# A decay-attention and two-expert-layer kernel: where TensorE is set back by one block, and when attention outputs leave PSUM

## The chip, the cores and the metric

The kernel runs on one core of a Trainium2 chip. The metric is the device time of one execution in microseconds (us); the figure for a kernel is the median of its runs. The core has five engines that work side by side, each through its own instructions in program order: TensorE (PE in the rows; PEld is its weight load), VectorE (DVE), ScalarE (ACT), GpSimd (POOL) and SyncE (SP), which here only issues the loads. They wait for one another through semaphores. SBUF is the working memory, PSUM the memory that TensorE writes.

## What is computed

An attention with a per-channel decay, then two mixture-of-experts layers on its output. Only the attention concerns us; cut to what matters:

```python
# q, k, v, f_logit: (4, 8, 768, 48)
f = 1.0 / (1.0 + np.exp(-f_logit))
for t in range(S):
    state = f[:, :, t, :, None] * state + np.einsum('bhd,bhe->bhde', k[:, :, t], v[:, :, t])
    y[:, :, t] = np.einsum('bhd,bhde->bhe', q[:, :, t], state)
x = attn_out.transpose(0, 2, 1, 3).reshape(3072, 384)
x = moe(x)      # expert = argmax of the gate logits, capacity 768, relu(x w1) w2
x = moe2(x)     # the same without capacity, with an output gate
```

## The kernel before

The attention is done in chunks of 128 positions. A **block** is one chunk of one batch with all 8 heads: 4 batches of 6 chunks, 24 blocks, numbered from 0. `c` is the chunk within its batch (block number modulo 6); the state that is carried from chunk to chunk is reset at c = 0 and not passed on at c = 5. Every block goes through these steps:

- `load(i)`: SyncE issues the load of the decays, q and k of block i into `fqk` (four buffers, so a load waits until block i-4 no longer needs its buffer, that is for kh(i-4)), and of v into `vt`.
- `decays(i)` and `starts(i)`: ScalarE takes the sigmoid of the block's decays into `f0` (line 605) and of each chunk's first position into `d1` (line 609).
- `elem(i)`: VectorE scans the running products `Pt` (line 615), takes a reciprocal, scans backward to `Qt` (line 622), and multiplies `qh` (line 627); GpSimd multiplies `kh` (line 630). Between them `tick` puts small VectorE jobs that route earlier groups of four blocks to experts (lines 316 to 354).
- `pe1(b)`: TensorE makes the scores of block b (line 638) and transposes kh (line 642); ScalarE copies both out of PSUM (`AT`, line 646, two copies; `kT`, line 649); GpSimd masks `AT` (line 647).
- `pe2(b)`: TensorE sums y (lines 660 and 676) and the state (lines 667 and 670); VectorE scales the state (`St`, line 679); ScalarE copies y out of PSUM to `yT` (line 682).
- `pe3(b)`: TensorE turns yT into token rows and gate logits (line 694); ScalarE copies the rows (`xrow`, line 695), VectorE reduces the logits (line 534).

One loop over i = 0 to 27 (iterations, counted from 0) writes these down, and the order in which they are written is the order on each engine (a manual schedule). Iteration i holds, in this order: `load(i+2)`, `elem(i)`, `decays(i+1)`, splits of expert weights that are due, then for the block `b` that the next line picks `pe1(b)`, `starts(i+1)`, `pe3(b-2)`, `pe2(b-1)`; then GpSimd's scatters of routed rows, and in the last iterations the transposes `xj` of the first expert's rows.

```python
b = i - 1 if i <= LAG else NBLK + 2 if i == LAG + 1 else i - 2
```

So TensorE first follows `elem` by one block; in iteration LAG+1 it gets no block at all; after that it follows by two. With `LAG = 3` the empty iteration is i = 4. TensorE's own order (block after block pe1, pe3, pe2) doesn't depend on LAG; what depends on it is where the ScalarE, VectorE and GpSimd instructions of these steps stand among those of `elem` and `decays`.

After the loop the rows of the first expert go through `layers` (lines 1065 and 1093), and the rest of the kernel is expert layers, TensorE work almost throughout.

Of the kernel before, what the change touches and what calls it, by code (L numbers as in the profile page):

```python
# [51 lines left out]
PMIN = 1e-30  # L52
PTHR = 1e-20
GROUP = 4
LAG = 3
CHOOSE, MEASURE = 2, 3
PACE, PACE2, TAIL, TAIL1 = (4, 2, 4, 4), (10, 3, 4, 4), (12, 0), (1, 4)
WT0, XT0 = (8, 10), [9, 9, 9]
# [7 lines left out]
def moe_attention_kernel(ctx: ExitStack, tc, blk, vblk, iw1, iw2, w1a, w2a, w1b, w2b, cap, out):  # L66
    nc = tc.nc
    V, A, G, PE = nc.vector, nc.scalar, nc.gpsimd, nc.tensor
# [31 lines left out]
    def psum_y(shape):  # L100
        return py.tile(shape, F32, name="pys", tag="pys")

    def psum_t(shape):
        return pt.tile(shape, F32, name="ptr", tag="ptr")
# [65 lines left out]
    def consts_load():  # L170
        nc.sync.dma_start(out=iw1_s, in_=iw1)
        nc.sync.dma_start(out=cap_i, in_=cap[0:1, 0:1].to_broadcast([128, 1]))
# [73 lines left out]
    def tick(n=1):  # L246
        for _ in range(n):
            if bg and not hasattr(bg[0], "on_pe"):
                bg.pop(0)()

    def tick_pe():

        if bg and hasattr(bg[0], "on_pe") and not bg[0].on_pe:
            bg.pop(0)()

    def tick_end():
        if bg and hasattr(bg[0], "on_pe"):
            bg[0].on_pe = False
# [283 lines left out]
    def attention():  # L542
        with ExitStack() as ac:
# [31 lines left out]
            st = {}  # L575
# [3 lines left out]
            def pace():  # L579
                return 4 if now[0] >= NBLK else 2 if rush or len(bg) > 12 else 1  # L580

            def load(i):
                t = Slot()
                x = ap.tile([HD, 3 * 512], F32, name="fqk", tag="fqk", bufs=4)
                t.v = ap.tile([128, 512], F32, name="vt", tag="vt", bufs=6)
                if i > 3:
                    nc.sync.dma_start(out=x, in_=blk[i])
                else:
                    for j in range(3):
                        nc.sync.dma_start(out=x[:, j * 512:(j + 1) * 512], in_=blk[i, :, j * 512:(j + 1) * 512])  # L590
                t.f, t.q, t.k = (x[:, j * 512:(j + 1) * 512] for j in range(3))
                st[i] = t
                if i:
                    load_v(i - 1)
                if i == NBLK - 1:
                    load_v(i)

            def load_v(i):
                nc.sync.dma_start(out=st[i].v, in_=vblk[i])

            def decays(i):
                t = st[i]
                ff = f0[i % 2]
                f4 = t.f.rearrange("p (a b) -> p a b", b=C)
                A.activation(out=ff[:, :512].rearrange("p (a b) -> p a b", b=C)[:, :, 1:],
                             in_=f4[:, :, 1:], func=AF.Sigmoid)

            def starts(i):
                A.activation(out=d1[:, 0::C], in_=st[i].f[:, 0::C], func=AF.Sigmoid)

            def elem(i):
                t = st[i]
                ff = f0[i % 2]
                Pt = ap.tile([HD, 512], F32, name="Pt", tag="Pt")
                V.tensor_tensor_scan(out=Pt, data0=ff[:, :512], data1=d1, initial=0.0,  # L615
                                     op0=ALU.mult, op1=ALU.add)
                tick(pace())
                t.pc = pcs[:HD, i * NP:(i + 1) * NP]
                V.tensor_scalar(out=t.pc, in0=Pt[:, C - 1::C], scalar1=PMIN, scalar2=None, op0=ALU.max)
                V.reciprocal(out=d1[:, ::-1][:, C - 1::C], in_=t.pc)  # L620
                Qt = ap.tile([HD, 512], F32, name="Qt", tag="Qt")
                V.tensor_tensor_scan(out=Qt[:, ::-1], data0=ff[:, 512:0:-1], data1=d1,
                                     initial=0.0, op0=ALU.mult, op1=ALU.add)
                tick(pace())
                t.qh = ap.tile([HD, 512], F32, name="qh", tag="qh", bufs=4)
                t.kh = ap.tile([HD, 512], F32, name="kh", tag="kh", bufs=3)
                V.tensor_tensor(out=t.qh, in0=t.q, in1=Pt, op=ALU.mult)  # L627
                tick(pace())

                (V if i < 2 else G).tensor_tensor(out=t.kh, in0=t.k, in1=Qt, op=ALU.mult)  # L630
# [21 lines left out]
            def pe2(i):  # L652
                t = st[i]
                c = i % NC
                S0, S1 = St[i % 2], St[(i + 1) % 2]
                y = psum_t([HD, NP, C])
                for p in range(NP):
                    for h in range(2):
                        u = 2 * p + h
                        PE.matmul(y[h * 64:h * 64 + (64, D)[h], p], lhsT=t.v[:, u * 64:u * 64 + (64, D)[h]],  # L660
                                  rhs=t.AT[h][:, p], start=(p == 0), stop=(c == 0 and p == NP - 1))
                heads = [(h, slice(h * 64, h * 64 + D), slice(h * 64, h * 64 + (64, D)[h])) for h in range(2)]
                if c < NC - 1:
                    sp = psum_y([HD, NP, D])
                    if c:
                        for h, hs, hw in heads:
                            PE.matmul(sp[hw], lhsT=ident[:HD, hw], rhs=S0, start=True, stop=False)
                    for p in range(NP):
                        for h, hs, hw in heads:
                            PE.matmul(sp[hw, p], lhsT=t.kT[:, p, hw],  # L670
                                      rhs=t.v[:, (2 * p + h) * 64:(2 * p + h) * 64 + D],
                                      start=(c == 0 and p == 0), stop=(p == NP - 1))
                if c:
                    for p in range(NP):
                        for h, hs, hw in heads:
                            PE.matmul(y[hs, p], lhsT=S0[hs, p], rhs=t.qh[hs, p * C:(p + 1) * C],  # L676
                                      start=False, stop=(p == NP - 1))
                if c < NC - 1:
                    V.tensor_tensor(out=S1, in0=sp, in1=t.pc.unsqueeze(2).to_broadcast([HD, NP, D]), op=ALU.mult)
                tick(pace())  # L680
                t.yT = ap.tile([HD, NP, C], F32, name="yT", tag="yT")
                A.copy(t.yT, y)

            def pe3(i):
                t = st[i]
# [60 lines left out]
            starts(0)  # L746
            decays(0)
            load(1)
            for i in range(NBLK + 4):
                now[0] = i  # L750
                if 2 <= i + 2 < NBLK:
                    load(i + 2)
                if i < NBLK:
                    elem(i)
                if i + 1 < NBLK:
                    decays(i + 1)
                if i == 0:
                    consts_load()
                if i < len(consts):
                    consts[i]()  # L760

                due = [p for p in wj if p[0] <= i]
                del wj[:len(due)]
                for _, f in due:
                    f()
                b = i - 1 if i <= LAG else NBLK + 2 if i == LAG + 1 else i - 2
                if 0 <= b < NBLK:
                    pe1(b)
                if i + 1 < NBLK:
                    starts(i + 1)  # L770
                tick_pe()
                if 0 <= b - 2 < NBLK:
                    pe3(b - 2)
                if 0 <= b - 1 < NBLK:
                    pe2(b - 1)
                if i >= hold:
                    scatters(2)
                if xj and i >= sincx:
                    xj.pop(0)()
                due = [p for p in wl if p[0] <= i]  # L780
                del wl[:len(due)]
                for _, f in due:
                    f()
                if ready.get("w") == i - 1:
                    steps = [0, 1, 2, 3, 4, 4, 5, 5, 6, 6, 7, 7]
                    wl = [(i + n, f) for n, f in zip(steps, W[0](0, 6) + W[0](1, 6))]
                    wj = [(i + n + 2, f) for n, f in zip(steps, split_jobs(0))]
                if ready.get("z") == i - 1:
                    early1.zeros(next(rows1), 5)
                if ready.get("x") == i - 1:  # L790
                    sincx = hold = i + 2
                    state["early"] = early1.rows(xs1, xearly)
                    xj = xt_jobs(state["early"])
                if i == NBLK:
                    flag()
                tick_end()
# [83 lines left out]
    class Plan:  # L880
# [143 lines left out]
        def next(self):  # L1024
            for t in (self.thr, self.row0, self.wrow):
                V.tensor_copy(self.turn, t)
                V.tensor_copy(t[:, :NOV - 1], self.turn[:, 1:])
# [408 lines left out]
```

## Time and profile before

| what | us |
|---|---|
| three timed runs | 635.26, 633.57, 635.64 |
| their median | 635.26 |
| the profiled execution's own time | 634.44 |
| its span, first to last instruction | 632.6 |
| busy in it: TensorE | 601.0 (95%) |
| VectorE | 394.0 (62%) |
| ScalarE | 319.8 (51%) |
| GpSimd | 160.3 (25%) |

The profiled execution is 0.82 us under the median, and 1.84 us of its time lie outside its span. The attention fills roughly the first 143 us of the span, and expert layers the rest. A busy TensorE in the profile is not the same as one at its peak; in the attention its instructions start back to back over long stretches, and that is what counts here. All positions below are us from the span's start.

### The profile page before, as it was taken

What the parts mean: (1) busy time and instruction counts of PE and PEld (TensorE: products, weight loads), DVE (VectorE), ACT (ScalarE), POOL (GpSimd) and SP (SyncE); (2) the same over time, 40 slices, a digit from 0 to 9 for tenths busy, and PEclk for the clock granted to TensorE, in tenths of its full rate; (3) what the DMA queues carried; (4) which work ended last, traced back from release to release, by engine and by line L of the source; (5) the groups of instructions that cost most, each with busy time, mean ns of one, the idle gap of its engine ahead of it and who ended that gap; (6) DMA issues with size and microseconds to landing.
All of it is one profiled execution on the core that took longest, in us unless ns stands there. A gap on an engine that the chain in (4) does not pass through costs nothing.

```text
span 632.6 us, 13955 instructions
## 1 busy us (share of the span) xinstructions
PE 601.0 (95%) x5240; PEld 579.9 (92%) x5240; DVE 394.0 (62%) x1075; ACT 319.8 (51%) x722; POOL 160.3 (25%) x219
## 2 busy tenths in 40 slices
PE   7799999988899999999999999999999999999990
PEld 7689888878899999999999999999999999999990
DVE  7778899947667474847567684544544454764520
ACT  3456665654545454544546354254554464665530
POOL 2556887655110102021120201120111010110120
PEclk9979999999999999999999999999999999999996
DMA  8997888548386273554554551285545344855210
GB/s 238 224 232 214 241 239 222 205 143 311 118 255 208 87 227 126 194 164 155 172 176 137 162 190 35 58 311 177 193 169 170 127 161 154 255 202 183 93 38 14
DMA packets 31532, 110.34 MB, mean 174 GB/s; under 512 B 4109, under 2 KB 15154, under 8 KB 27614
## 3 DMA queue, kind: packets, MB, share of 16 engines
q1 hardware_dynamic: 26158, 95.05, 49.4%
q0 software_dynamic: 5296, 14.30, 6.9%
q8 instruction: 43, 0.70, 0.5%
q14 instruction: 35, 0.29, 0.2%
HBM read 83.47 MB, written 26.21 MB: 173 GB/s over the span
## 4 chain that ended last, share of the span: by engine, by line
PE 51%; issue 29%; DVE 7%; POOL 5%; DMA 4%; ACT 2%; SPq 0%; POOLq 0%; DVEq 0%; ACTq 0%
PE pys L1093 18%; PE phs L1065 12%; PE pxs L1065 6%; POOL out L377 4%; DMA fqk<-blk 2%; PE ptr L660 2%; PE ptr L694 2%; PE phs L638 2%; PE ptr L676 2%; DVE Pt L615 2%; PE ptr L1115 1%; PE pys L1115 1%; PE phs L508 1%; DVE qh L627 1%; PE pys L670 1%
## 5 line engine op out<-in xcount | busy, mean ns | idle before, releaser
L1093 PE MATMUL pys<-hbuf,w2h 128*128 128x360 f32 (+10 forms) x864 | 206.5, 321 | 0.0
L1093 PEld LDWEIGHTS pys<-hbuf,w2h 128*128 128x128 f32 x864 | 149.8, 188 | 1.1
L1093 PE MATMUL pys<-hbuf,w2l 128*128 128x360 f32 (+10 forms) x432 | 137.8, 319 | 0.0
L377 POOL DMA_INDIRECT xs<-xrow,r_dest x53 | 55.0, 1038 | 204.3 <-DVE xl L510 85.9
L1065 PE MATMUL phs<-xh,w1h 128*128 128x312 f32 (+10 forms) x306 | 99.6, 325 | 1.7 <-DVE xl L510 1.0
L1065 PE MATMUL phs<-xl,w1h 128*128 128x312 f32 (+10 forms) x306 | 96.7, 316 | 0.0
L1065 PE MATMUL phs<-xh,w1l 128*128 128x312 f32 (+10 forms) x306 | 96.7, 316 | 0.0
L233 DVE TENSOR_TENSOR w2l<-raw,w2h 128x512 fp32r<-128x512 f32 x96 | 65.6, 687 | 45.6 <-ACT w2h L232 44.9
L233 DVE TENSOR_TENSOR w1l<-raw,w1h 128x512 fp32r<-128x512 f32 x96 | 65.3, 696 | 30.2 <-ACT w1h L232 29.6
L1093 PEld LDWEIGHTS pys<-hbuf,w2l 128*128 128x128 f32 x432 | 81.5, 189 | 0.5
L377 POOL DMA_INDIRECT out<-xrow,oid x31 | 30.3, 977 | 183.7 <-ACT xrow L1165 174.6
L1068 DVE SCALAR_TENSOR_TENSOR hbuf<-phs,hbuf 128x312 fp32r<-128x312 f32 (+10 forms) x102 | 50.8, 499 | 23.1 <-ACT hbuf L1067 22.2
L1067 ACT ACTIVATE hbuf<-phs 128x312 fp32r<-128x312 f32 (+10 forms) x102 | 46.1, 452 | 34.7 <-PE phs L1065 33.8
L1065 PEld LDWEIGHTS phs<-xh,w1h 128*128 128x128 f32 x306 | 57.7, 188 | 2.7 <-DVE xl L510 1.3
L232 ACT CAST w2h<-raw 128x512 fp32r<-128x512 f32 x96 | 59.3, 623 | 0.0
L232 ACT CAST w1h<-raw 128x512 fp32r<-128x512 f32 x96 | 57.7, 621 | 1.0 <-DMA raw<-w1a 1.0
L1065 PEld LDWEIGHTS phs<-xl,w1h 128*128 128x128 f32 x306 | 57.7, 189 | 0.4
L1065 PEld LDWEIGHTS phs<-xh,w1l 128*128 128x128 f32 x306 | 57.7, 189 | 0.3
L1099 ACT COPY ybuf<-pys 128x312 f32<-128x312 f32 (+4 forms) x27 | 11.7, 435 | 73.5 <-PE pys L1093 73.5
L1096 ACT CAST ybuf<-pys 128x360 fp32r<-128x360 f32 (+5 forms) x27 | 12.3, 455 | 72.2 <-PE pys L1093 72.2
L1065 PE MATMUL pxs<-xh,w1h 128*128 128x360 f32 (+10 forms) x150 | 48.8, 325 | 0.0
L1065 PE MATMUL pxs<-xl,w1h 128*128 128x360 f32 (+10 forms) x150 | 47.6, 317 | 0.0
(236 smaller groups left out, 1052.0 us busy)
## 6 DMA issues: line engine op xcount, KB each, us to landing
fqk<-blk SPq DMA_DIRECT2D x20, 672.0 KB, 5.6
raw<-w1b SPq DMA_DIRECT2D x8, 1536.0 KB, 7.9
raw<-w2b SPq DMA_DIRECT2D x8, 1536.0 KB, 6.9
raw<-w1a SPq DMA_DIRECT2D x7, 1536.0 KB
raw<-w2a SPq DMA_DIRECT2D x7, 1536.0 KB, 8.3
vt<-vblk SPq DMA_DIRECT2D x24, 256.0 KB, 7.2
xs<-zrow SPq DMA_DIRECT2D x5, 786.0 KB, 6.7
fqk<-blk SPq DMA_DIRECT2D x12, 224.0 KB, 5.7
```

What stands on the lines that cost most here:

```text
L232: A.copy(hi[:, c], raw[l][:, c])
L233: V.tensor_tensor(out=lo[:, c], in0=raw[l][:, c], in1=hi[:, c], op=ALU.subtract)
L377: G.indirect_dma_start(out=dst, out_offset=bass.IndirectOffsetOnAxis(ap=idx, axis=0), in_=src, in_offset=None, bounds_check=bound, oob_is_ ...
L615: V.tensor_tensor_scan(out=Pt, data0=ff[:, :512], data1=d1, initial=0.0, op0=ALU.mult, op1=ALU.add)
L638: PE.matmul(a[h][:, p], lhsT=t.kh[hs, p * C:(p + 1) * C], rhs=t.qh[hs, p * C:(p + 1) * C], start=True, stop=True)
L660: PE.matmul(y[h * 64:h * 64 + (64, D)[h], p], lhsT=t.v[:, u * 64:u * 64 + (64, D)[h]], rhs=t.AT[h][:, p], start=(p == 0), stop=(c == 0 and ...
L676: PE.matmul(y[hs, p], lhsT=S0[hs, p], rhs=t.qh[hs, p * C:(p + 1) * C], start=False, stop=(p == NP - 1))
L694: PE.matmul(ps[hc, p], lhsT=t.yT[:, p, hc], rhs=iw1_s[:, p], start=True, stop=True)
L1065: PE.matmul(ps, lhsT=w[:, c], rhs=x[:, k], start=(n == 0), stop=(n == 3 * KD - 1))
L1067: A.activation(out=hh[f], in_=ps, func=AF.Relu)
L1068: V.scalar_tensor_tensor(out=hl[f], in0=ps, scalar=0.0, in1=hh[f], op0=ALU.max, op1=ALU.subtract)
L1093: PE.matmul(ps, lhsT=w[:, c], rhs=x, start=(n == 0), stop=(n == 3 * KF - 1))
```

## The change

Two edits in `attention()`. `LAG` goes from 3 to 8, so TensorE follows by one block up to iteration 8, and the iteration without a block is i = 9. And the copy of y out of PSUM is taken out of `pe2`: a new function `leave(i)` holds it, and the loop calls it in the next iteration, right behind `decays`.

```diff
-LAG = 3
+LAG = 8
...
                 tick(pace())
+                t.y = y
+
+            def leave(i):
+                t = st[i]
                 t.yT = ap.tile([HD, NP, C], F32, name="yT", tag="yT")
-                A.copy(t.yT, y)
+                A.copy(t.yT, t.y)
...
+            out = []
             for i in range(NBLK + 4):
...
                 if i + 1 < NBLK:
                     decays(i + 1)
+                if out:
+                    leave(out.pop())
                 if i == 0:
...
                 if 0 <= b - 1 < NBLK:
                     pe2(b - 1)
+                    out.append(b - 1)
```

What it moves is seen on ScalarE in iterations 2 to 5. In these rows f0 is written by `decays` (L605), d1 by `starts` (L609); numbers behind names tell one buffer use from another. Before, from `starts(3)` on:

```order
L609 ACTIVATE d1_189<-fqk_270 112x4
L682 COPY yT_372<-ptr_353 112x512
L605 ACTIVATE f0_0_184<-fqk_313 112x4x127
L646 COPY AT_407<-phs_391 128x512
L646 COPY AT_408<-phs_392 128x512
L649 COPY kT_406<-pys_401 128x448
L609 ACTIVATE d1_189<-fqk_313 112x4
L695 COPY xrow1_93<-ptr_415 128x384
L682 COPY yT_455<-ptr_426 112x512
L605 ACTIVATE f0_1_185<-fqk_374 112x4x127
L609 ACTIVATE d1_189<-fqk_374 112x4
L605 ACTIVATE f0_0_184<-fqk_457 112x4x127
```

The same place now:

```order
L609 ACTIVATE d1_189<-fqk_270 112x4
L605 ACTIVATE f0_0_184<-fqk_313 112x4x127
L686 COPY yT_387<-ptr_353 112x512
L646 COPY AT_407<-phs_391 128x512
L646 COPY AT_408<-phs_392 128x512
L649 COPY kT_406<-pys_401 128x448
L609 ACTIVATE d1_189<-fqk_313 112x4
L699 COPY xrow1_93<-ptr_415 128x384
L605 ACTIVATE f0_1_185<-fqk_372 112x4x127
L686 COPY yT_470<-ptr_426 112x512
L646 COPY AT_491<-phs_475 128x512
L646 COPY AT_492<-phs_476 128x512
```

yT(0) (the first yT row) stood ahead of `decays(4)` and now stands behind it, yT(1) now stands behind `decays(5)`, and the copies AT(3) follow there at once, where they used to stand behind `decays(6)`.

On VectorE the state and logits of a block now fall between the scans of the next ones in iterations 4 to 8. Before, after qh(4):

```order
L184 TENSOR_SCALAR capr_109<-base0_113,cap_f_108 128x8
L615 SCALAR_TENSOR_TENSOR Pt_480<-f0_1_185,d1_189 112x512
L619 TENSOR_SCALAR pcs_110<-Pt_480 112x4
L620 RECIPROCAL d1_189<-pcs_110 112x4
L622 SCALAR_TENSOR_TENSOR Qt_484<-f0_1_185,d1_189 112x512
```

Now:

```order
L184 TENSOR_SCALAR capr_109<-base0_113,cap_f_108 128x8
L534 TENSOR_REDUCE pmt_190<-ptr_499 128x8
L679 TENSOR_TENSOR St_1_192<-pys_519,pcs_110 112x192
L615 SCALAR_TENSOR_TENSOR Pt_543<-f0_1_185,d1_189 112x512
L619 TENSOR_SCALAR pcs_110<-Pt_543 112x4
```

Pt(5) now stands behind the logits of block 1 and the state of block 2. In iteration 9 there is neither; from iteration 10 on VectorE's order is the same as before, except that three of the routing jobs of blocks 0 to 3 have been done earlier. SyncE's order is unchanged.

At the end of the attention ScalarE's order, before, then now (xh is the first expert's first transposed rows, the yT is that of block 23):

```order
L695 COPY xrow0_92<-ptr_2362 128x384
L682 COPY yT_2393<-ptr_2373 112x512
L509 CAST xh_95<-phs_2401 128x256
L232 CAST w2h0_88<-raw2_91 128x512 x2
L695 COPY xrow0_92<-ptr_2412 128x384
```

```order
L699 COPY xrow0_92<-ptr_2362 128x384
L509 CAST xh_95<-phs_2399 128x256
L686 COPY yT_2406<-ptr_2373 112x512
L232 CAST w2h0_88<-raw2_91 128x512 x2
L699 COPY xrow0_92<-ptr_2412 128x384
```

yT(23) has moved behind the first xh.

## Rows read from the trace of the kernel before

**Rows 1.** Stretches: length, busy PE, PEld, DVE, ACT, POOL; clock, DMA, GB/s.

```profile
39.70:75.00 35.30, 35.30 (x607) 31.66 (x605) 30.13 (x69) 23.20 (x51) 24.83 (x49) 1.00 0.86 228
75.00:122.00 47.00, 45.19 (x732) 40.17 (x731) 43.63 (x113) 30.46 (x69) 34.11 (x39) 0.96 0.82 237
165.00:632.60 467.60, 452.52 (x3062) 446.64 (x3060) 260.53 (x740) 227.53 (x515) 63.10 (x75) 0.99 0.49 158
```

**Rows 2.** TensorE in order of time: start, length, line, in brackets idle time and releaser.

```profile
12.76 1.16 PE L638 MATMUL phs<-qh,kh 48*128 48x128 f32 x16 [2.29 <-DVE kh L630]
17.60 1.16 PE L638 MATMUL phs<-qh,kh 48*128 48x128 f32 x16 [1.67 <-POOL kh L630]
19.22 0.93 PE L694 MATMUL ptr<-iw_s,yT 112*64 112x104 f32 x16
...
22.74 1.16 PE L638 MATMUL phs<-qh,kh 48*128 48x128 f32 x16
...
30.98 2.09 PE L638 MATMUL phs<-qh,kh 48*128 48x128 f32 x16 [3.03 <-issue]
...
39.71 1.16 PE L638 MATMUL phs<-qh,kh 48*128 48x128 f32 x16
...
44.85 1.16 PE L638 MATMUL phs<-qh,kh 48*128 48x128 f32 x16
...
49.23 1.16 PE L638 MATMUL phs<-qh,kh 48*128 48x128 f32 x16
...
53.18 1.16 PE L638 MATMUL phs<-qh,kh 48*128 48x128 f32 x16
```

**Rows 3.** ScalarE in order of time, iterations 2 to 5 and the attention's end.

```profile
16.87 0.61 ACT L682 COPY yT<-ptr 112x512 f32<-112x512 f32 x1
20.92 0.63 ACT L605 ACTIVATE f<-fqk 112x508 f32<-112x508 f32 x1 [3.44 <-DMA fqk<-blk]
21.45 1.06 ACT L646 COPY AT<-phs 128x512 f32<-128x512 f32 x2
...
29.79 0.63 ACT L605 ACTIVATE f<-fqk 112x508 f32<-112x508 f32 x1 [2.79 <-DMA fqk<-blk]
30.32 1.05 ACT L646 COPY AT<-phs 128x512 f32<-128x512 f32 x2
...
141.48 0.59 ACT L682 COPY yT<-ptr 112x512 f32<-112x512 f32 x1 [1.45 <-PE ptr L676]
141.97 0.38 ACT L509 CAST xh<-phs 128x256 fp32r<-128x256 f32 x1
142.23 1.15 ACT L232 CAST w2h<-raw 128x512 fp32r<-128x512 f32 x2
```

**Rows 4.** Stretches as in rows 1, around the two falls of TensorE's clock.

```profile
31.00:39.70 8.70, 8.70 (x88) 7.57 (x88) 6.09 (x14) 4.29 (x11) 5.75 (x8) 0.61 1.03 218
110.00:114.00 4.00, 3.88 (x47) 3.66 (x47) 3.69 (x7) 2.83 (x7) 2.88 (x4) 0.57 1.00 324
```

**Rows 5.** VectorE in order of time.

```profile
43.97 0.36 DVE L679 TENSOR_TENSOR St<-pys,pcs 112x192 f32<-112x192 f32 x1 [0.78 <-PE pys L670]
...
44.57 1.21 DVE L615 TENSOR_TENSOR_SCAN Pt<-f,d 112x512 f32<-112x512 f32 x1
...
53.30 0.36 DVE L679 TENSOR_TENSOR St<-pys,pcs 112x192 f32<-112x192 f32 x1 [0.55 <-PE pys L670]
...
53.67 1.21 DVE L615 TENSOR_TENSOR_SCAN Pt<-f,d 112x512 f32<-112x512 f32 x1
...
57.23 0.19 DVE L322 SCALAR_TENSOR_TENSOR pmt<-pmt,r_ks 128x32 f32<-128x32 f32 x1
```

**Rows 6.** GpSimd in order of time: kh(8).

```profile
47.67 1.67 POOL L630 TENSOR_TENSOR kh<-fqk,Qt 112x512 f32<-112x512 f32 x1 [2.24 <-PE ptr L694]
```

**Rows 7.** VectorE's waits from 54 to 76: who for whom, total, times, longest.

```profile
DVE St L679 <- PE pys L670: 1.6, 3, 0.9
```

**Rows 8.** The same from 75 to 122.

```profile
DVE St L679 <- PE pys L670: 0.4, 1, 0.4
```

## The prediction

> **What bounds the kernel now.** I read the stretches first, because the change touches the attention alone. From 165 on TensorE is busy 452.5 of 467.6 us in expert layers that the change leaves as they are [rows 1]; whatever is won must arrive at the end of the attention. There the stretches from 39.7 to 75 and from 75 to 122 differ. In the first TensorE has no gap at all and VectorE rests 5.2 us; in the second VectorE is busy 43.6 of 47.0 us and TensorE rests 1.8 us [rows 1]. So TensorE paces up to about 75 and VectorE from there. VectorE's waits say the same: 1.6 us for TensorE's state sums between 54 and 76, in three places, then only 0.4 us up to 122 [rows 7, 8]. A gain of TensorE in the first stretch is thus worth at most what VectorE still waits for it; behind that, VectorE's own work is the floor.
>
> Then TensorE's early order. It idles 2.29 us before block 1 and 1.67 us before block 2, and 3.03 us before block 4 at 30.98 [rows 2]. That last hole is a matter of ScalarE's order: the copies AT(3), which free the PSUM that block 4 needs, run at 30.32 behind `decays(6)`, which waited for its load until 29.79 [rows 3]. After the hole block 4 runs slowly: its scores take 2.09 us instead of 1.16, and block 5 follows 8.73 us later, where 39.71 to 44.85 is 5.14 [rows 2]. The granted clock is 0.61 over these 8.7 us, which at the two levels of 2.4 and 1.2 GHz makes 6.8 us at the lower one (0.39 of 8.7 us, over 0.5) [rows 4]. The hole and the slow stretch are what the change can take away.
>
> **The change part by part.** *The copy of y.* yT(0) ran at 16.87, before `decays(4)`. Now it stands behind it, and `decays(4)` starts at 20.92, when its load lands; the next ScalarE instruction starts 0.53 later (21.45) and a yT takes 0.61 [rows 3]. So yT(0) is done at 22.06, and TensorE's pe3(0), which ran at 19.22 [rows 2], starts at 22.1: a new hole of 2.9 us. Queued behind it is all of TensorE.
>
> *LAG.* From there TensorE's order is the old one. pe3(0) to block 3's first matmul is 3.52 us (19.22 to 22.74), so block 3 starts at 25.6, 2.9 us late. AT(3) now stands behind `decays(5)` and not `decays(6)`, so nothing holds block 4. If the clock stays up, blocks 4, 5 and 6 follow at 5.14 us each: 30.8, 35.9, 41.0, against 30.98, 39.71 and 44.85 before. The next two steps hold a last and a first chunk and are shorter: 4.38 to block 7 (44.85 to 49.23), so 45.4, and 3.95 from there to block 8 (49.23 to 53.18) [rows 2].
>
> That holds only if the inputs come. With a lag of one, VectorE starts Pt(i+1) behind the state of block i-2. The state St(4) comes 0.88 before block 6's first matmul (43.97 against 44.85), now 40.2; Pt(7) is 0.60 later (43.97 to 44.57), 40.8; kh is complete 4.77 after its Pt (44.57 to 47.67 plus 1.67), 45.5 [rows 2, 5, 6]. Block 7 can start at 45.5 and not 45.4, and block 8 at 49.5, 3.7 us ahead of 53.18. The margin is nothing, but it costs only 0.1.
>
> VectorE meanwhile loses by being tied to TensorE. St(6) comes 0.12 after block 8's first matmul (53.30 against 53.18), so 49.6, and Pt(9) 0.37 behind it (53.30 to 53.67): 50.0. Iteration 9 has neither state nor logits: from a Pt to the end of L322 is 3.75 (53.67 to 57.42), so Pt(10) starts at 53.7 [rows 5]. Before it started at 53.67. **VectorE is level, TensorE is 3.7 us ahead.** From here the order on both is as before, and three things differ. Three routing jobs are already done; the one with a row takes 0.19, and as instructions overlap a little I take 0.4 for three. The waits of 1.6 us in 54 to 76 vanish, being smaller in total than TensorE's lead [rows 7]. The wait of 0.4 in 75 to 122 [rows 8] should go too.
>
> *The last copy.* yT(23) ran at 141.48 ahead of xh at 141.97; now xh comes first, when its matmuls are through, at about 141.8, yT(23) 0.26 later (141.97 to 142.23) at 142.1 instead of 141.48, and w2h starts 0.3 later than 142.23 [rows 3]. ScalarE is what the end of the attention hangs on here, so this costs 0.3 (bounds 0 and 0.6, the delay of yT itself). In the iterations between, `decays` ahead of yT moves 0.6 us of ScalarE work in front of a copy that in the second half still waits for TensorE, and costs nothing; without that cover it would cost those 0.6 a block.
>
> *The loads.* A load waits for kh four blocks earlier. In iterations 4 to 8 kh comes later by no more than the new hole, 2.9 us, and so do the loads behind it. Each is wanted three iterations afterwards, 13 us at 4.38 each, so I take nothing.
>
> Sum, against the execution's own 634.44 us: Pt(10) 0.0, jobs -0.4, waits -1.6 and -0.4, last copy +0.3: -2.1, so 632.3. Bounds: with neither jobs nor the 0.4 and the dearer copy -1.0; with Pt(10) a further 1.0 earlier (the margins above are that coarse) -3.1. The median of the three runs is 0.82 above that execution, so the changed kernel's median is put at 633.2, with 632.2 to 634.3 for this case.
>
> **Rivals.** *B: the clock falls in the new hole.* The hole of 3.03 us was followed by the lower clock; those of 2.29 and 1.67 were not, and the clock also fell near 110, where TensorE is busy 3.88 of 4.00 us [rows 2, 4]. The new hole is 2.9 us, with only block 2's 1.6 us of work between it and the 1.67 us hole. So this is near even. Price: the stretch of 110 to 114, at 0.57 over 4.0 us, has 3.4 us at 1.2 GHz, half of it lost, 1.7; the one after 30.98 lost 8.73 less 5.14, 3.6 [rows 2, 4]. VectorE is tied to TensorE until Pt(9), so all of it arrives: -2.1 plus 1.7 to 3.6 is -0.4 to +1.5, that is 634.9 to 636.8 on the scale of the median, middle 635.9. **At its dearer end the change is slower**, from the point where the lower clock costs more than 2.1 us of TensorE work. The Trainium skill speaks for this rival: "TensorE: Matmul & The Clock Gate", section "What's actually happening", says that "the default state is throttled, and activity releases the throttle". By that rule taken strictly the change swaps one hole for another of the same length; the trace agrees for the hole at 30.98 and not for the two before it.
>
> *C: VectorE owns the pace.* If VectorE's waits come back elsewhere (on GpSimd, or on ScalarE's copies behind `starts`), TensorE's lead buys nothing: 0 plus the 0.3 of the last copy, 635.6. For it: 43.6 of 47.0 us busy from 75 on [rows 1]. Against it: the three waits before 76 are plain.
>
> *D: one block of lag starves TensorE.* kh(7) is on time by nothing. If VectorE or GpSimd takes 0.5 longer in each of iterations 4 to 8, block 8 is 2.5 us later, Pt(10) too: +0.4 on the sum, 635.7.
>
> **How the numbers follow.** A, as summed, 0.45; B 0.35; C 0.1; D 0.1. The forecast is A: 633.2. The range takes A's cheap side, 632.0, and B to its upper end, 636.8; about 2 in 10 lie outside. A measurement of this kernel tells about 0.3%, 1.9 us, from no change: faster is below 633.35, slower above 637.2. Of A somewhat over half is below that line, of the others little: faster 0.30. Slower is the edge of B and D together with what I haven't seen, 0.13. Same is the rest, 0.57.
>
> **What would show it.** In the trace of the changed kernel: TensorE's pe3(0) at about 22.1 behind yT(0) at 21.5, not 19.2; no idle time of 3 us before block 4, which starts near 30.8; the granted clock from 22 to 40, at 1.00 for A and below it for B; block 8's first matmul near 49.5; Pt(10) near 53.7; no wait of St for TensorE from 54 to 76; yT(23) behind the first xh. If Pt(10) comes much before 53, my tie of VectorE to TensorE is wrong and the gain is larger; if the waits vanish and VectorE is not about 2 us earlier by 75, it is slowed by something else. If the first loads land at other times than 20.9, the new hole has another size, and the sum moves with it.

## The result, and the profile after

The changed kernel is **slower**: 639.47 us as the median of five runs against 635.00 for the kernel before beside it, ratio 1.0086 (95% interval 1.0064 to 1.0108). A second set gave 1.0087 (1.0071 to 1.0103). The forecast was 633.2 with a range up to 636.8, so it fails on the sign, and the range on its upper end.

The profiled execution took 641.16 us with a span of 639.2. Its stretches, to be read beside [rows 1] (length, busy PE, PEld, DVE, ACT, POOL; clock, DMA, GB/s):

```profile
39.70:75.00 35.30, 32.93 (x517) 28.54 (x515) 29.36 (x63) 19.32 (x44) 23.42 (x50) 0.95 0.75 205
75.00:122.00 47.00, 45.11 (x730) 40.11 (x730) 42.19 (x106) 28.83 (x65) 34.03 (x38) 0.97 0.82 235
165.00:639.20 474.20, 459.01 (x3112) 452.61 (x3110) 267.16 (x755) 233.03 (x530) 65.33 (x79) 0.99 0.49 157
```

Behind 165 there are 6.6 us more: the attention ends later, and what follows is the same work. In the stretch to 75 TensorE now rests 2.4 us, where it had no gap. TensorE in order of time, beside [rows 2] (start, length, line, in brackets idle time and releaser), shows where:

```profile
12.89 2.42 PE L638 MATMUL phs<-qh,kh 48*128 48x128 f32 x16 [1.64 <-DVE kh L630]
...
24.20 1.65 PE L698 MATMUL ptr<-iw_s,yT 112*64 112x104 f32 x16 [3.14 <-ACT yT L686]
...
30.51 1.16 PE L638 MATMUL phs<-qh,kh 48*128 48x128 f32 x16
...
54.70 1.16 PE L638 MATMUL phs<-qh,kh 48*128 48x128 f32 x16 [0.19 <-POOL kh L630]
...
59.84 1.16 PE L638 MATMUL phs<-qh,kh 48*128 48x128 f32 x16
...
63.28 0.94 PE L698 MATMUL ptr<-iw_s,yT 112*64 112x104 f32 x16 [1.74 <-ACT yT L686]
...
68.88 1.16 PE L638 MATMUL phs<-qh,kh 48*128 48x128 f32 x16
```

pe3(0) (L698, line 694 before) idles 3.14 us for yT(0), and then runs at 1.65 instead of 0.93 us. Block 3 starts at 30.51 instead of 22.74. There is no hole before block 4 any more; it starts at 35.66, 5.15 us behind block 3. A second loss stands between block 9 (59.84) and block 10 (68.88): 9.04 us instead of 5.15. ScalarE, beside [rows 3], shows the cause of the first:

```profile
23.05 0.63 ACT L605 ACTIVATE f<-fqk 112x508 f32<-112x508 f32 x1 [4.74 <-DMA fqk<-blk]
23.58 0.57 ACT L686 COPY yT<-ptr 112x512 f32<-112x512 f32 x1
24.04 1.08 ACT L646 COPY AT<-phs 128x512 f32<-128x512 f32 x2
```

`decays(4)` waited 4.74 us for its load, and yT(0) behind it with it. The granted clock in the stretches around the two places, beside [rows 4]:

```profile
12.00:20.00 8.00, 7.11 (x62) 6.51 (x64) 5.10 (x9) 3.80 (x10) 4.30 (x6) 0.57 1.06 239
24.00:30.00 6.00, 5.80 (x62) 5.50 (x64) 1.13 (x3) 2.74 (x7) 1.32 (x3) 0.50 1.04 226
64.00:68.00 4.00, 3.97 (x44) 3.37 (x42) 3.01 (x6) 1.74 (x5) 2.20 (x3) 0.57 0.99 267
```

0.50 is the lower of the two levels, 1.2 GHz. It holds for all of 24 to 30 behind the new hole, and for most of 64 to 68 behind the second one. The low clock from 12 to 20 lies ahead of everything that the change moves. VectorE, beside [rows 5], carries the delay on, from Pt(10) and Pt(13):

```profile
58.59 1.21 DVE L615 TENSOR_TENSOR_SCAN Pt<-f,d 112x512 f32<-112x512 f32 x1
...
75.32 0.36 DVE L679 TENSOR_TENSOR St<-pys,pcs 112x192 f32<-112x192 f32 x1 [1.76 <-PE ptr L676]
75.60 1.21 DVE L615 TENSOR_TENSOR_SCAN Pt<-f,d 112x512 f32<-112x512 f32 x1
```

Pt(10) is 4.9 us late (53.67 before), Pt(13) 7.6 (68.00), and Pt(23) 7.85 (130.13 against 122.28). So nearly all of it is lost by 76, in two places.

### The profile page after: what moved, and what is told of

The parts are those of the page before. It is cut to its first block, busy times and chain, and to the rows that moved or that the text cites. A ratio compares the mean times of both kernels' runs of the same rounds, so it can differ in the third digit from the quotient of the medians.

```text
span 639.2 us, 13955 instructions
## 1 busy us (share of the span) xinstructions
PE 609.0 (95%) x5240; PEld 586.7 (92%) x5240; DVE 395.3 (62%) x1075; ACT 319.6 (50%) x722; POOL 160.5 (25%) x219
## 4 chain that ended last, share of the span: by engine, by line
PE 51%; issue 29%; DVE 6%; POOL 5%; DMA 4%; ACT 2%; SPq 0%; POOLq 0%; DVEq 0%; ACTq 0%
PE pys L1101 18%; PE phs L1073 13%; PE pxs L1073 6%; POOL out L377 4%; DMA fqk<-blk 3%; PE ptr L660 3%; PE ptr L698 2%; DVE Pt L615 2%; PE ptr L676 2%; PE ptr L1123 1%; PE phs L638 1%; PE pys L1123 1%; DVE Qt L622 1%; PE pys L670 1%; PE phs L508 1%
## 5 line engine op out<-in xcount | busy, mean ns | idle before, releaser
L377 POOL DMA_INDIRECT xs<-xrow,r_dest x53 | 54.8, 1034 | 204.9 <-DVE xl L510 64.7
L377 POOL DMA_INDIRECT out<-xrow,oid x31 | 30.3, 979 | 183.6 <-ACT xrow L1173 174.5
L1073 PE MATMUL pxs<-xh,w1l 128*128 128x360 f32 (+10 forms) x150 | 47.5, 317 | 0.0
```

Source lines behind the costliest of these rows:

```text
L377: G.indirect_dma_start(out=dst, out_offset=bass.IndirectOffsetOnAxis(ap=idx, axis=0), in_=src, in_offset=None, bounds_check=bound, oob_is_ ...
L1073: PE.matmul(ps, lhsT=w[:, c], rhs=x[:, k], start=(n == 0), stop=(n == 3 * KD - 1))
```

## The experiments

All ratios are to runs of the kernel before on the same chip, with 95% intervals. "Held" means that no scatter is issued in iteration 10; why, is told at those runs. The table gathers what one profile of each kernel shows (us from the span's start; the hole is TensorE's idle time before pe3(0), or before pe3(1) where that is said). A profile is one execution and the ratio is that of medians, and the two need not go together: the executions profiled with a hole before pe3(1) took longer than the median of their kernel (640.32 us with a median of 636.81, 637.40 with 634.33, 636.43 with 635.18), and the changed kernel's second one was shorter (632.61 with 637.56). So the profiles show mechanisms, and how large a loss is on the whole only the ratios say.

| kernel | ratio | decays(4) | hole | block 3 | Pt(10) | Pt(13) | Pt(23) |
|---|---|---|---|---|---|---|---|
| before | 1 | 20.92 | none | 22.74 | 53.67 | 68.00 | 122.28 |
| before, second profile | | 21.39 | none | 22.94 | 53.61 | 67.94 | 121.71 |
| changed | 1.0086 | 23.05 | 3.14 | 30.51 | 58.59 | 75.60 | 130.13 |
| changed, second profile | 1.0087 | 19.87 | none | 24.76 | 52.84 | 67.93 | 121.44 |
| LAG alone | 1.0020 | 20.99 | none | 26.20 | 54.27 | 71.28 | 124.79 |
| copy alone | 1.0050 | 19.58 | 1.07 | 24.25 | 53.63 | 68.21 | 123.75 |
| changed, yT(0) early | 1.0040 | 22.15 | 1.66, pe3(1) | 23.34 | 53.58 | 70.55 | 124.99 |
| changed, yT(7) early | 1.0069 | 19.36 | none | 24.36 | 52.43 | 69.39 | 124.97 |
| changed, held | 1.0061 | 21.45 | 3.23 | 28.37 | 56.44 | 71.00 | 124.74 |
| held, hole filled | 1.0043 | 22.05 | 1.65 | 26.73 | 54.80 | 69.26 | 124.61 |
| held, yT(0) early | 1.0021 | 22.77 | 2.27, pe3(1) | 24.32 | 56.40 | 70.88 | 126.13 |
| held, yT(0), yT(7) early | 1.0032 | 22.58 | 1.34, pe3(1) | 23.78 | 55.34 | 70.40 | 124.94 |
| held, yT(0), yT(1) early | 1.0010 | 21.57 | none | 23.26 | 52.21 | 65.95 | 119.72 |
| LAG alone, held | 1.0000 | 20.69 | none | 23.30 | 51.93 | 65.66 | 120.05 |
| LAG alone, held, again | 0.9988 | 21.86 | none | 23.27 | 52.51 | 66.24 | 120.88 |

### The two edits apart

LAG alone leaves the copy of y in `pe2`:

```diff
-LAG = 3
+LAG = 8
```

> LAG = 8, with the copy of y left at the end of pe2 (line 682) as before. Theory 1 (the late copy makes the loss: it puts pe3(0) behind decays(4) and its load, and TensorE's clock falls around that hole): pe3(0) is back near 19.2, the hole of 3 us before block 4 is gone too, and LAG alone is a gain: 630 to 634. Theory 2 (LAG makes the loss: with one block of lag VectorE and TensorE wait for each other, and the empty iteration, now i = 9, makes a hole in TensorE's work there whatever the copy does): 636 to 640, with a hole of 1 to 2 us on TensorE near pe3(7). Theory 3 (the slow clock from 12.9 to 20 and the later first loads in the profile of the changed kernel are an accident of that one execution): this run's clock up to 20 need not look like that one's.

Measured: 1.0020 (1.0002 to 1.0039). pe3(0) ran at 20.65 without a hole, and the hole before block 4 was gone. The hole near pe3(7) of Theory 2 was there, 1.22 us. There was no gain, and Pt(13) was 3.3 us late. The granted clock fell early here too, to 0.50 from 16 to 24, where no engine's order differs yet from that of the kernel before.

The copy alone is the changed kernel with the old lag:

```diff
-LAG = 8
+LAG = 3
```

> The copy of y moved behind the next decays, LAG = 3 as before. Theory 1: pe3(0) 3 us late, the old hole before block 4 still there: 637 to 640. Theory 2: the late copy alone costs little, since the hole before block 4 takes up what pe3(0) loses: 634 to 636.

Measured: 1.0050 (1.0032 to 1.0068). So the copy makes the larger part of the loss and LAG a smaller one; neither theory is right alone. Together they give what the changed kernel shows (0.20% and 0.50%, against 0.86%), within the intervals. Where the copy alone loses its 0.50% its profile doesn't show: what pe3(0) loses is taken up, as Theory 2 has it, where TensorE waits anyway for what stands behind `decays(6)` (block 5 starts at 39.67 and Pt(10) at 53.63, as before), and Pt(23) is 1.5 to 2.0 us late by losses behind Pt(13), where executions of one kernel differ as well.

### One copy put back

The changed kernel with one copy at the end of `pe2` again, for yT(0), and in another kernel for yT(7), ahead of whose pe3 the second hole stands:

```diff
                 t.y = y
+                if i in (0,):
+                    leave(i)
...
-                    out.append(b - 1)
+                    if b - 1 not in (0,):
+                        out.append(b - 1)
```

> The changed kernel, but yT(0) alone is copied at the end of pe2(0), as before; every other copy stays behind decays. Theory 1: this takes the hole of 3.14 us before pe3(0) away, and with it most of the loss: 632 to 635. Theory 2: the hole goes, but TensorE only waits later, and the hole near pe3(7) stays: 636 to 639.

> The changed kernel, but yT(7) alone, the copy before which the iteration without a block lies, is copied at the end of pe2(7). In the changed kernel's trace it ran at 62.65 behind starts(11) and decays(12), and TensorE idled 1.74 us before pe3(7). Starts(11) waits for Qt(10) in either place, so the early copy can take only 0.5 of these 1.74 us. Theory 1: 639, less than 1 us gained, since the loss lies at pe3(0). Theory 2: the same unless the clock stays up in 64 to 68 (0.57 there in the changed kernel): then 636 to 637.5.

Measured: yT(0) early 1.0040 (1.0015 to 1.0064), yT(7) early 1.0069 (1.0048 to 1.0090). yT(0) alone is worth about 0.47%, over half of the loss. For yT(7) the difference is not beyond the intervals. With yT(0) back, TensorE idled 1.66 us one block later, before pe3(1), in the execution profiled; that is taken up below.

### The scatters that came early

LAG alone still cost 0.2%, and its trace showed a thing that the prediction had overlooked. GpSimd of LAG alone, in order of time (L630 is kh, L647 the masks of AT, L377 the scatters of routed rows):

```profile
57.37 1.64 POOL L630 TENSOR_TENSOR kh<-fqk,Qt 112x512 f32<-112x512 f32 x1 [1.64 <-PE pys L642]
...
59.24 1.22 POOL L647 TENSOR_SCALAR_AFFINE_SELECT AT<-AT 128x512 f32<-128x512 f32 x2
62.10 1.69 POOL L377 DMA_INDIRECT xs<-xrow,r_dest  x1 [1.64 <-DVE Qt L622]
64.09 0.99 POOL L377 DMA_INDIRECT xs<-xrow,r_dest  x1 [0.30 <-issue]
65.09 1.30 POOL L630 TENSOR_TENSOR kh<-fqk,Qt 112x512 f32<-112x512 f32 x1
...
66.55 1.27 POOL L647 TENSOR_SCALAR_AFFINE_SELECT AT<-AT 128x512 f32<-128x512 f32 x2
```

kh(11) starts at 65.09 behind two scatters, where Qt(11) was done at 62.03; the masks of AT(9) follow at 66.55, and TensorE waits for them:

```profile
67.30 0.43 PE L660 MATMUL ptr<-AT,vt 128*64 128x128 f32 x2 [1.52 <-POOL AT L647]
```

In the kernel before these two scatters stand one iteration later, behind kh(11) and the masks of AT(9):

```profile
61.59 1.58 POOL L630 TENSOR_TENSOR kh<-fqk,Qt 112x512 f32<-112x512 f32 x1 [1.71 <-PE ptr L694]
...
63.39 1.22 POOL L647 TENSOR_SCALAR_AFFINE_SELECT AT<-AT 128x512 f32<-128x512 f32 x2
...
64.94 1.31 POOL L377 DMA_INDIRECT xs<-xrow,r_dest  x1 [0.19 <-issue]
```

With LAG = 8 the three routing jobs that are done earlier finish the first routing an iteration earlier, and the loop then issues its scatters at the end of iteration 10. The edit that holds them back, on LAG alone and on the changed kernel:

```diff
-                if i >= hold:
+                if i >= hold and i != LAG + 2:
```

> LAG = 8 alone (copy of y at the end of pe2), and in iteration 10 no scatter is issued, so that GpSimd's first two scatters stand where they stood before the change, behind kh(11) and the masks of AT(9). With LAG = 8 the first routing is done an iteration earlier and its scatters moved ahead of kh(11); there TensorE waited 1.52 us for the masks of AT(9), and kh(11) came at 65.09 where Qt(11) was done at 62.03. Theory S (the scatters moved early make LAG's loss): that wait goes, and with it 1.5 to 2.5 us: 0.2 to 0.4% faster than LAG alone, ratio to the kernel before 0.997 to 1.000. Theory E (the empty iteration makes it: TensorE has drained and each step behind it waits for elem(10) and elem(11), with or without scatters): at most 0.5 us, ratio 1.001 to 1.003.

> The changed kernel, both edits, with the same scatters held back from iteration 10. Theory S: 1.5 to 2.5 us faster than the changed kernel. Theory E: within 0.5 us of it.

Measured: 1.0000 (0.9985 to 1.0014) and 1.0061 (1.0039 to 1.0084), against 1.0020 and 1.0087 without. That is 0.20% and 0.26% less, 1.3 and 1.6 us: Theory S rather than Theory E, near S's lower end. Each pair of intervals overlaps; what speaks for S is that both pairs go the same way, that a third one does below (yT(0) early, 1.0040 without and 1.0021 with the hold), and the trace. In LAG alone, held, GpSimd reads:

```profile
59.82 1.57 POOL L630 TENSOR_TENSOR kh<-fqk,Qt 112x512 f32<-112x512 f32 x1 [1.71 <-issue]
...
61.62 1.22 POOL L647 TENSOR_SCALAR_AFFINE_SELECT AT<-AT 128x512 f32<-128x512 f32 x2
...
63.16 1.31 POOL L377 DMA_INDIRECT xs<-xrow,r_dest  x1 [0.19 <-issue]
```

kh(11) starts 0.14 us behind Qt(11)'s end (59.68) instead of 3.06, and the 1.52 us wait for the masks of AT(9) is gone. Theory E's loss is there as well: block 10 follows block 9 by 2.5 us more than 5.14, 1.2 us of it a hole at pe3(7). VectorE waits for no state between 54 and 76 in this kernel, so it doesn't hold VectorE up.

### Both kernels once more

> The changed kernel unaltered, a second time and beside the others. If the slow clock from 12.9 to 20 us and the late first loads of its first profile are an accident, this profile shows other times for them and the time stays 4 to 5 us above the kernel before; if they belong to the change, they are seen again.

> The kernel before, unaltered, for a second profile: the granted clock from 12 to 24 and from 30 to 40 us, and the start of decays(4). In its first profile the clock was full up to 31, and decays(4) started at 20.92. The four kernels with one or both edits all had a fall between 12 and 24. If this one has it too, that fall is no part of the change.

Measured: the changed kernel again 1.0087, with runs from 632.61 to 638.74, where the first five lay between 638.24 and 641.16 (the kernel before took 632.41 beside these and 635.00 beside the first). The profile is that of the quickest run, 632.61, and it shows why that one was quick (ScalarE, then TensorE):

```profile
19.87 0.63 ACT L605 ACTIVATE f<-fqk 112x508 f32<-112x508 f32 x1 [2.83 <-DMA fqk<-blk]
20.41 0.57 ACT L686 COPY yT<-ptr 112x512 f32<-112x512 f32 x1
```

```profile
19.04 1.74 PE L638 MATMUL phs<-qh,kh 48*128 48x128 f32 x16
21.24 0.93 PE L698 MATMUL ptr<-iw_s,yT 112*64 112x104 f32 x16
24.76 1.16 PE L638 MATMUL phs<-qh,kh 48*128 48x128 f32 x16
```

The load landed at 19.87, and TensorE was itself late, its clock having fallen in block 1: pe3(0) finds yT(0) ready, there is no hole, and Pt(23) is no later than before. So the late copy costs where the load lands behind TensorE, 19.4 to 23.1 us in the profiles of the table, and that differs from execution to execution. The kernel before, a second time, has no fall of the clock from 12 to 24, but the hole and the fall before block 4 as in [rows 2]:

```profile
30.95 2.52 PE L638 MATMUL phs<-qh,kh 48*128 48x128 f32 x16 [2.72 <-issue]
39.65 1.16 PE L638 MATMUL phs<-qh,kh 48*128 48x128 f32 x16
```

Whether the falls between 12 and 20, seen in every profile of a kernel with an edit except one (the changed kernel, held) and in neither of the kernel before, belong to the edits isn't settled: up to 16 us no engine's order differs, and in the kernels with LAG alone none does up to 26.

### Hole, clock, and the copies behind the first

yT(0) early with scatters held:

> The changed kernel with scatters held back in iteration 10 and yT(0) alone copied at the end of pe2(0) as before. The runs so far put the losses at 0.45% for yT(0) (1.0087 less 1.004), 0.25% for the early scatters (1.0087 less 1.0061). If they add up, this is 1.001 to 1.003 of the kernel before; if yT(0) only delays what another wait takes up later, it stays near 1.006.

Measured: 1.0021 (1.0004 to 1.0038), as it should be if the two losses add up. What was left shows in its trace, on ScalarE and on TensorE (the added lines make L698 L700):

```profile
27.21 0.63 ACT L605 ACTIVATE f<-fqk 112x508 f32<-112x508 f32 x1 [1.94 <-DMA fqk<-blk]
27.75 0.56 ACT L688 COPY yT<-ptr 112x512 f32<-112x512 f32 x1
```

```profile
28.37 0.94 PE L700 MATMUL ptr<-iw_s,yT 112*64 112x104 f32 x16 [2.27 <-ACT yT L688]
```

```profile
30.00:32.00 2.00, 2.00 (x28) 1.82 (x25) 0.75 (x2) 0.77 (x2) 1.83 (x4) 0.50 1.08 230
```

The same mechanism one block later: yT(1) behind `decays(5)`, which waits for the next load; a hole of 2.27 us, and the lower clock behind it.

> As the run beside it, but yT(0) and yT(7) are both copied at the end of pe2, ahead of decays. If the copy's loss is only at the two places where decays waits longer than TensorE can, this equals LAG alone with scatters held, 0.9985 to 1.0015 of the kernel before, and the copies of the other 22 blocks cost nothing. If every late copy costs its 0.6 us of ScalarE, it stays above 1.003.

Measured: 1.0032 (1.0015 to 1.0049). The expectation that it equals LAG alone is missed, since yT(1) was left late here too (a hole of 1.34 us).

To part the hole from the clock, TensorE repeats work in the hole:

```diff
-                for p in range(NP):
+                for p in list(range(NP)) * (6 if i == 2 else 1):
                     PE.transpose(ktp[:, p], t.kh[:, p * C:(p + 1) * C], ident[:HD, :HD])
```

> The changed kernel with scatters held back in iteration 10, and TensorE repeats the transposes of kh(2) (line 642) five times more: 20 matmuls, some 2.7 us at the full clock by their 0.53 us for four, in the hole before pe3(0). yT(0) is as late as before, so the hole's own 3.2 us stay; only what the lower clock takes behind it can be won. Theory K (the clock falls because TensorE idles in the hole, and costs 2.2 us from pe3(0) to block 3): the clock stays at 1.00 there, 1.5 to 2.5 us less, ratio 1.002 to 1.004. Theory H (the hole itself is the loss, or the clock falls all the same): ratio 1.005 to 1.008.

Measured: 1.0043 (1.0025 to 1.0060). TensorE of the held kernel without the repeats:

```profile
22.60 1.65 PE L698 MATMUL ptr<-iw_s,yT 112*64 112x104 f32 x16 [3.23 <-ACT yT L686]
...
28.37 1.16 PE L638 MATMUL phs<-qh,kh 48*128 48x128 f32 x16
```

and with them (x24 are the 24 transposes):

```profile
19.04 2.52 PE L642 MATMUL pys<-ident,kh 112*128 112x112 f32 x24
23.21 0.93 PE L698 MATMUL ptr<-iw_s,yT 112*64 112x104 f32 x16 [1.65 <-ACT yT L686]
...
26.73 1.16 PE L638 MATMUL phs<-qh,kh 48*128 48x128 f32 x16
```

From pe3(0) to block 3 it takes 3.52 us instead of 5.77, the same as in [rows 2] at the full clock, and the granted clock from 22 to 28 is 1.00 instead of 0.55:

```profile
22.00:28.00 6.00, 4.79 (x86) 4.38 (x87) 2.25 (x6) 4.13 (x10) 2.01 (x3) 1.00 1.02 217
```

So in the trace the clock costs 2.25 us behind this hole, and with TensorE kept busy this is saved: Theory K. That is one execution of each; a hole of 1.65 us is left in it, and behind the holes before pe3(1) of about that length the clock stayed up once (1.66 us, 1.00 from 28 to 32) and fell once (1.34 us, 0.62). The time, 1.0043, lies between the two theories' ranges; the gain of 0.18% is within the intervals. The Trainium skill, "TensorE: Matmul & The Clock Gate", section "What's actually happening", has it that the throttled state is the default and activity releases it; this pair agrees.

Without an empty iteration at all:

```diff
-LAG = 3
+LAG = 30
```

> LAG = 30, the copy of y at the end of pe2: TensorE follows elem by one block to the end and no iteration is without a block. Theory E (the empty iteration costs TensorE its lead, 2.5 us between blocks 9 and 10 even with scatters held): VectorE is floor from there, the attention's end comes one block's tail sooner, 2 to 4 us faster than before, 0.994 to 0.998. Rival: with one block of lag kh comes too late for TensorE once VectorE paces, TensorE idles in every block and its clock falls: 1.00 to 1.02.

Measured: 1.0044 (1.0023 to 1.0064); the rival is right. Who waited for whom from 76 to 140 (total, times, longest), and TensorE's stretch:

```profile
PE phs L638 <- POOL kh L630: 6.0, 4, 2.3
```

```profile
76.00:122.00 46.00, 41.57 (x680) 37.06 (x678) 39.49 (x105) 28.43 (x63) 31.88 (x36) 0.96 0.81 239
```

With one block of lag kh comes too late once VectorE paces: the kernel before has no such wait there, and TensorE rests 4.4 of 46 us. It waits in four of the blocks and not in every one, and the granted clock, 0.96, is no lower than in [rows 1]. This kernel was not run with scatters held, and they stand ahead of kh(11) in it too (kh(11) starts at 63.63, Qt(11) ends at 62.08), so a part of the 0.44% can be theirs. If it is as much as above, some 0.2% is left, within the interval: that the second block of lag is worth the empty iteration is likely from the waits, but the time alone doesn't show it.

### What is left when both causes are taken out

> The changed kernel with scatters held back in iteration 10, and yT(0) and yT(1) both copied at the end of pe2, ahead of decays(4) and decays(5); the other copies stay late. With yT(0) alone early, TensorE idled 2.27 us before pe3(1) instead of pe3(0), since yT(1) then waits behind decays(5) for the next load, and 1.0021 was measured; LAG alone with scatters held gave 1.000. Theory W (the wait for a load only moves to the next copy that stands behind decays): no hole before pe3(1), decays(6) finds its load landed, and the ratio is 0.9985 to 1.0015. Rival: each late copy costs a little everywhere; then 1.002 to 1.003 stays.

> LAG = 8 alone with scatters held back in iteration 10, again, beside the other: the version with neither loss. 0.9985 to 1.0015 was measured; the same is expected. In its first profile Pt(23) came 1.7 to 2.2 us before the two profiles of the kernel before; if that is a gain of the version and not of the execution, 0.996 to 0.998.

Measured: the changed kernel, held, with yT(0) and yT(1) in their old place, 1.0010 (0.9990 to 1.0029): within Theory W's range. From the changed kernel down to it the steps are 1.0087, 1.0061 (held), 1.0021 (yT(0) early) and 1.0010. pe3(1) has no hole, and what the other 22 late copies cost is not told from nothing; with 0.9988 for the run beside it, it could be 0.2%:

```profile
19.74 0.93 PE L700 MATMUL ptr<-iw_s,yT 112*64 112x104 f32 x16
...
24.89 0.94 PE L700 MATMUL ptr<-iw_s,yT 112*64 112x104 f32 x16
```

LAG alone, held: 0.9988 (0.9970 to 1.0006), after 1.0000. In both of its profiles Pt(23) is 0.8 to 2.2 us earlier than in the two of the kernel before. The timed medians are 0.5 and 0.6 us lower, no more than no difference. No version beats the kernel before by what these runs can tell.

## Why the prediction was wrong, point by point

**The new hole: right in kind, and its cost unlike what was forecast.** pe3(0) was forecast at 22.1 with 2.9 us of hole. Where the load landed near the 20.92 of the kernel before (21.45, changed kernel held) it came at 22.60 with 3.23 us. The forecast named the landing of the load as a condition, and it moves: 23.05 in the first profile, 19.87 in the second, where there was no hole and the time, 632.61, was that of the kernel before.

**The clock: the wrong case was taken.** Case A, at 0.45, let the clock stay up; it fell behind the hole, rival B at 0.35. B's price of 1.7 to 3.6 us was sized well, 2.25 us in the held kernel (5.77 less 3.52) and 2.8 in the first profile (30.51 less 24.20 is 6.31, less 3.52).

**B's sum failed all the same**, and this is the first failed step: it put B's price on top of A's gain of 2.1 us. In the changed kernel, held, block 8 starts at 52.55 against 53.18, a lead of 0.6 us instead of 3.7, and VectorE, tied to TensorE until Pt(9), starts Pt(10) at 56.44, 2.8 us late. The waits of 1.6 us that A was to save were to be paid out of that same lead; 1.0 us of waits was still there. The rows of that kernel (TensorE, VectorE, VectorE's waits from 54 to 76):

```profile
52.55 1.16 PE L638 MATMUL phs<-qh,kh 48*128 48x128 f32 x16 [0.19 <-POOL kh L630]
...
57.69 1.16 PE L638 MATMUL phs<-qh,kh 48*128 48x128 f32 x16
...
66.47 1.16 PE L638 MATMUL phs<-qh,kh 48*128 48x128 f32 x16
```

```profile
56.44 1.22 DVE L615 TENSOR_TENSOR_SCAN Pt<-f,d 112x512 f32<-112x512 f32 x1
```

```profile
DVE St L679 <- PE pys L670: 1.0, 2, 0.5
```

The loss of 2.8 at Pt(10) is 2.5 and 3.0 at Pt(23) against the two profiles of the kernel before.

**"From here the order on both is as before" is the second failed step.** "Both" are TensorE and VectorE; the order on GpSimd was not looked at. Three routing jobs done earlier were entered as a gain of 0.4; through them the scatters moved ahead of kh(11) at the place where TensorE has just lost its lead, and cost 1.3 to 1.6 us. The term had the wrong sign.

**Nothing was entered for yT(1).** It moved behind `decays(5)` in the same rows of the order as AT(3). In the changed kernel its wait is covered by the loss at yT(0); with yT(0) put back it shows, with 1.3 to 2.3 us of hole in three profiles, all of executions longer than their median. In the ratios it is 0.1% (1.0021 to 1.0010), within the intervals.

**The empty iteration was entered at nothing, the third failed step.** A TensorE 3.7 us ahead was not to wait there, and was to keep its lead behind it. In the changed kernel, held, block 10 follows block 9 8.78 us later (57.69 to 66.47), which puts TensorE from 0.6 us ahead of the kernel before to 3.0 behind (63.47 there). The kernel with the filled hole comes nearest to case A, for its clock stays at 1.00 from 20 to 76: its block 8 is 2.3 us early (50.92), but block 10 follows block 9 by 7.67 us (56.06 to 63.73), the lead is gone, and VectorE still waits 1.8 us for states from 54 to 76. So A's gain does not come where the clock stays up either.

In LAG alone, held, the step is also 7.67 us (53.19 to 60.86). There VectorE did not feel it: its state waits from 54 to 76 vanished as forecast, and Pt(13) came at 65.66 and 66.24 instead of 68.00. But about 1.5 us came back on VectorE itself, in L619 (last section).

**What held.** The hole before block 4 and the low clock behind it were indeed a matter of AT(3) behind `decays(6)`: with LAG = 8 both are gone (in the two profiles of LAG alone, held, TensorE idles 0.2 and 0.8 us from 24 to 36, at a clock of 1.00). The last copy costs 0.3 us: w2h starts 10.06 us behind block 23's first matmul (134.93 to 144.99, changed kernel held) and not 9.76 (132.47 to 142.23). From block 3 to block 8 it took 24.18 us (28.37 to 52.55) where 23.9 were forecast, so rival D cost 0.3 us and not 2.5. Rival C, at 0.1, describes what is left when the causes found are taken out: 1.0010, 1.0000 and 0.9988 are the time of C, in which TensorE's lead buys nothing, and not A's 2 us less. L619's longer times are one place where VectorE lost it again; that they are the only one isn't shown.

## What to carry to other kernels

A copy that another engine needs should not stand behind an instruction that waits for a load, for the wait is then both engines', and an order of instructions that leaves no hole in one execution leaves one of 3 us in another, when the load lands behind TensorE. When a change makes some engine's small jobs finish earlier, look at every queue that they release work into: here that was two scatters which then stood in front of the critical product. And a lead can be spent once: a rival's price, and what an iteration without work costs, must be taken from the lead before the gains that hang on it are counted.

## What the runs showed of the hardware

TensorE's clock falls at other places in other executions of the same kernel: from 76 to 122 the granted clock of the kernel before is 0.96 in its first profile and 1.00 in its second. After the hole of the empty iteration (56 to 72 us) it fell in six of the twelve profiles with LAG = 8 (0.89) and stayed up in six (1.00).

VectorE's small L619 (112x4 elements, 0.17 us at its quickest) took up to 1.93 us when it met GpSimd's work (LAG alone, from 64.69, with kh(11) on GpSimd from 65.09 to 66.39). In LAG alone, held, it started at 57.34 and ended at 58.14, and the masks on GpSimd ended at 58.11 (VectorE, then GpSimd):

```profile
57.34 0.80 DVE L619 TENSOR_SCALAR pcs<-Pt 112x4 f32<-112x4 f32 x1
```

```profile
56.90 1.21 POOL L647 TENSOR_SCALAR_AFFINE_SELECT AT<-AT 128x512 f32<-128x512 f32 x2
```

From 56 to 76 the four L619 together took 3.03 us there and 1.53 in the kernel before (3.05 and 1.52 in the second profiles). The Trainium skill, "SBUF — State Buffer", section "SBUF: two separate sides", says that VectorE's faster modes and GpSimd share one pair of ports, that whichever starts first has it for its whole instruction and that the other is blocked; these rows fit that. Which mode L619 runs in no run here shows. Why the first scatter of LAG alone starts only 1.64 us after the masks, at the end of Qt(11), isn't settled.
